# Linear attention and two MLPs in one program: batch 7's attention moved into a pair of the second layer, and q's products of batches 2 to 6 in three float32r passes

## The chip, the cores and the metric

The kernel is one program on one core of a Trainium2 chip. A core has a matrix engine (TensorE, PE in the rows; PEld is its weight load), a vector engine (VectorE, DVE), a scalar engine (ScalarE, ACT), GpSimd (POOL) and SyncE (SP), which here issues most of the DMAs. The metric is the time of one execution on the device in microseconds (us); lower is better.

## What is computed

Eight batches of eight heads, 576 tokens of 64 columns each, go through a linear attention with a root-mean-square norm. Its result, 4608 x 512, goes through two MLPs of width 2048:

```python
kv = einsum('bhsd,bhse->bhde', k, v)
out = einsum('bhsd,bhde->bhse', q, kv)
x = out / sqrt(mean(out*out, -1) + 1e-6) * g_norm     # heads side by side: 4608 x 512
h = x @ w_in1;  g = where(h >= 1, h, where(h <= -1, 0, (h + 1)**2 / 4));  x = g @ w_out1
r = maximum(x @ w_in2, 0);  out = (r*r) @ w_out2
```

## The kernel before

**Number formats.** q, k, v and x are float32. A large product is made of three float32r passes: each operand is split into a high part (a cast, mostly on ACT) and a low part (the rest, a subtraction on DVE), and high times high, high times low and low times high are summed (`mm3`, `mm_group`). A matmul on float32 operands needs no parts and takes longer.

**The MLPs.** A block is one layer of one batch, 512 of its tokens; the 64 left over of all eight batches make one more batch, the ninth. Blocks of layer 1 for batches 0 to 4 go through both matrices (`h_stage`, `g_stage`, `out_stage`), batches 5 and 6 only through the first (`h_stage`). From there on two batches are one *pair*, n = 0 to 5: `PAIRS` holds (1,5), (2,0), (2,2), (1,7), (2,4), (2,6), the layer and the first batch. A pair's matrix product is done by Strassen's scheme in Winograd's form, with seven products of half size in the order 1, 6, 2, 7, 5, 4, 3. Each pair has a first phase (`in_phase`: four q of seven products of two tiles of 6 matmuls, tiles `ph`, matrix w_in) and a second one (`out_phase`: seven products of 8 steps, tiles `po`, matrix w_out). Weights come ready in DRAM (`wsd`), one `ws` tile for each product, loaded by SP through a ring of eight buffers, so some products ahead. The results of a second layer's pair (`ov`, four of them, `outputs`) are transposed on DVE and stored by SP, eight DMAs each; they are written in the next pair's first phase, at steps 0, 1, 5 and 9 of its 28 (`late`). x of the pair after is loaded and split by jobs in the second phase (`x2_jobs`).

**The attention.** Two heads form a head pair, four head pairs a batch. For each: `load_kv` and `load_q` (SP: k, v, their last 64 rows as `rest`, and q in four DMAs), `kv_stage` (k times v on PE, two head pairs at a time, copied into the two diagonal blocks of `kvbd`), `t_stage` (transpose of q on DVE), `o_stage` (PE: q times kv, two halves of 288 tokens, then squares and scaling on ACT, the low part of the square on DVE), `r_stage` (PE: sums of squares by `ones`, two halves `pr`; ACT: logarithm, exponential, square; DVE: a Newton step for each half and the norm). Batch 1 uses three passes for q times kv; batches 2 to 7 use one matmul in float32 on q as it is transposed. The result becomes x of the MLP. For batch 7, whose MLP comes late, it is kept in DRAM (`keep_x`: `xpd`, and `xrd` for the 64 tokens left over).

**What sets the order.** The program is written as one list. Blocks are steps of `h_stage`; attention and the preparation of weights hang on them as hooks at numbered half steps. `STARTS` gives the starting slot s of each head pair of the list `order`; `attention` puts the loads at s - 7, kv and transpose at s, the halves at s + 3 and s + 4, the norm at s + 6. In the list before, batch 7's head pairs stand among those of batches 4, 5 and 6. In pairs there is no attention. A scheduler then orders each engine's instructions by their readiness in its own model; on the chip every engine executes its list in that order, and waits with all that is behind where an operand isn't there. Tiles live in rings and tagged buffers: a tile that takes over a buffer waits for the last reader of the one before, a store included.

Of the kernel before, what the change touches and what calls it, by code (L numbers as in the profile page):

```python
# [76 lines left out]
def linear_attention_rms_two_mlps(  # L77
# [12 lines left out]
    nc = tc.nc  # L90
# [18 lines left out]
    STARTS = (32, 39, 46, 53, 60, 66, 72, 78, 84, 90, 96, 102, 109, 115, 121, 127, 133, 139)  # L109
    STARTS += (145, 151, 156, 161, 166, 173)  # L110
# [30 lines left out]
    PAIRS = [(1, PLAIN), (2, 0), (2, 2), (1, B - 1), (2, 4), (2, 6)]  # L141
    LAST_B = B - 1
# [59 lines left out]
    kvbd = [const.tile([P, P], F32, name=f"kvbd{i}") for i in range(2)]  # L202
    kv1 = const.tile([P, 2, P], F32R, name="kv1")
# [271 lines left out]
    def kv_stage(*pairs):  # L475
        ps = bank(pairs[0][0], "pkv_{}_{}".format(*pairs[0]))
        for n, (b, hp) in enumerate(pairs):
            kt, vt = kvm.pop((b, hp))
            r = kvr.pop((b, hp))


            for c in range(MR + 1):
                for j in range(2):
                    s = slice(j * D, (j + 1) * D)
                    d = slice(n * P + j * D, n * P + (j + 1) * D)
                    lhs, rhs = (kt[:, c, j], vt[:, j, c, :]) if c < MR else (r[0][:, j], r[1][:, j])
                    nc.tensor.matmul(ps[s, d], lhs, rhs, start=c == 0, stop=c == MR)  # L487
        for n, (b, hp) in enumerate(pairs):
            for j in range(2):
                s = slice(j * D, (j + 1) * D)  # L490
                d = slice(n * P + j * D, n * P + (j + 1) * D)
                if b == 0:
                    copy(engine("kv_hi", b), kv0[s, hp, s], ps[s, d])
                    continue
                if (b, hp) in WHOLE:
                    copy(engine("kv_hi", b), kvw[s, hp % 2, s], ps[s, d])
                    continue
                if b > 1:
                    copy(engine("kv_hi", b), kvbd[turn[b, hp] % len(kvbd)][s, s], ps[s, d])
                    continue  # L500
                t = kv1
                copy(engine("kv_hi", b), t[s, 0, s], ps[s, d])
                nc.vector.tensor_tensor(t[s, 1, s], ps[s, d], t[s, 0, s].bitcast(F32), ALU.subtract)
# [56 lines left out]
    def t_stage(b, hp):  # L560
        work = [ap1.tile([P, S], F32, tag=f"wk{n}", name=f"wk{n}_{b}_{hp}") for n in range(2)]
        if b > 1 or (b, hp) in WHOLE:
            qT = ap1.tile([P, S], F32, tag="hl0", name=f"qT_{b}_{hp}")
            nc.vector.transpose(qT, qs.pop((b, hp)))
            hl[b, hp] = (work, qT)
            return
        qT = ap1.tile([P, S], F32, tag="wk2", name=f"qf_{b}_{hp}")
        parts = [ap1.tile([P, S], F32R, tag=f"hl{n}", name=f"qT{n}_{b}_{hp}") for n in range(2)]
        nc.vector.transpose(qT, qs.pop((b, hp)))
        copy(engine("q_hi", b), parts[0], qT)  # L570
        engine("q_lo", b).tensor_tensor(parts[1], qT, parts[0].bitcast(F32), ALU.subtract)
        hl[b, hp] = (work, parts)

    def o_stage(b, hp, half):
# [15 lines left out]
        if b > 1:  # L590
            nc.tensor.matmul(  # L591
                ps[:, :U], kvbd[turn[b, hp] % len(kvbd)], parts[:, c], start=True, stop=True
            )
        else:
            mm3(ps[:, :U], lambda a: kv1[:, a, :], lambda a: parts[a][:, c], True, True)
# [8 lines left out]
    def r_stage(b, hp):  # L604
# [24 lines left out]
        xt = st.tile([P, TB], F32, tag="st", name=f"xt_{hp}")  # L629
        nc.vector.scalar_tensor_tensor(t, t, -3.0, y, op0=ALU.add, op1=ALU.mult)  # L630
        nc.vector.tensor_tensor(xt, o[:, :TB], t[:, :TB], ALU.mult)
        xr = ap1.tile([P, REM], F32, tag="xr", name=f"xr_{hp}")
        nc.vector.tensor_tensor(xr, o[:, TB:], t[:, TB:], ALU.mult)
        x_kept[hp] = xt, xr
# [3 lines left out]
    def keep_x(b, hp):  # L638
        xt, xr = x_kept.pop(hp)
        nc.sync.dma_start(xpd[:, hp, :], xt)  # L640
        nc.sync.dma_start(xrd[:, hp, b, :], xr)
# [26 lines left out]
    def attention(starts, order):  # L668

        slots = []  # L670
        for j, (s, (b, hp)) in enumerate(zip(starts, order)):
# [3 lines left out]
            elif j % 2 == 0:  # L675
                two = order[j : j + 2]
                turn[two[1]] = len(turn)
                slots += [(max(0, s - 7), load_kv, *i) for i in two]
                slots.append((s, kv_stage, *two))
            slots += [  # L680
                (max(0, s - 7), load_q, b, hp),
                (s, t_stage, b, hp),
                (s + 3, o_stage, b, hp, 0),
                (s + 4, o_stage, b, hp, 1),
# [138 lines left out]
    t1_ring = Ring(*[(st, "st")] * 7, (dt, "dt3"))  # L823
    v_ring = Ring(*((wp, f"w0_{i}") for i in (12, 13)))
# [110 lines left out]

    FIRST = (1, 6, 5)
# [4 lines left out]
    def in_phase(n):  # L941
# [6 lines left out]
        for q in range(NQ):  # L948
            ps = {}
            e = {}  # L950
            for p in PRODUCTS:
                w = take_w2(layer(n), 0, q, p)
                for i in range(2):
# [11 lines left out]
                    if p == 1:  # L965
                        e[i, 1] = tile(e_ring, f"e1_{n}_{k}")
# [4 lines left out]
                    elif p in (6, 7):  # L971
                        kind = "e16" if p == 6 else "e167"
                        if p == 6:
                            e[i, 6] = tile(e_ring, f"{kind}_{n}_{k}")
                        else:
                            e[i, 7] = tile(e_ring, f"{kind}_{n}_{k}")
# [147 lines left out]
    def outputs(n, hn, hm):  # L1124
# [7 lines left out]
        t = (t_ring if n < NS - 1 else v_ring).tile([P, 2, TB], F32, f"ov{n}_{hn}_{hm}")  # L1132
# [96 lines left out]
    for t in kvbd + [kv1.bitcast(F32)]:  # L1229
        nc.vector.memset(t, 0.0)  # L1230
# [135 lines left out]
```

## Time and profile before

| | |
|---|---|
| runs | 1554.84, 1554.6, 1552.7 us; median 1554.6 |
| the profiled execution's own time | 1553.93 us |
| its span in the trace | 1552.2 us |
| the blocks end, pair 0's second phase begins | 630.16 us |
| pair 2, the second layer's second: first phase | 858.64 to 934.80 us |
| pair 2: second phase | 934.80 to 1010.96 us |
| granted clock of PE over the span | 1.00 |

All times in rows are from the start of the span. A row of the timeline joins instructions of the same kind that follow each other; xN is how many. In brackets stands how long the engine had stood idle before, and which instruction ended that. An L number is a line of the kernel's file, 246 being `mm3`, 927 `mm_group`, 591 the float32 product in `o_stage`, 487 `kv_stage` and 843 `load_w2`.

### The profile page before, as it was taken

The page shows a single profiled execution, that of the slowest core. Times are in us where ns is not written, and L with a number is a line of the kernel's source. Part 1 is how long each engine was busy: PE and PEld are TensorE (multiplying, and loading weights), DVE is VectorE, ACT ScalarE, POOL GpSimd, SP SyncE. Part 2 cuts the span into 40 slices and gives each one's busy share as a digit, 9 for nine tenths or more (in the row PEclk, how much of TensorE's full clock was granted, in tenths as well). Part 3 has the DMA queues.
Part 4 walks back from the last instruction along what each step waited for, and adds up shares of the span by engine and source line. Part 5 has one row for each costly group of instructions (what it writes and reads, how often), then busy time and mean ns, then how long its engine had stood idle before and what let it go on. Part 6 is the DMA issues. An engine that isn't in the chain of part 4 may idle for free.

```text
span 1552.2 us, 22204 instructions
## 1 busy us (share of the span) xinstructions
PE 1541.5 (99%) x7631; PEld 1274.0 (82%) x7633; DVE 1140.9 (74%) x1991; ACT 971.2 (63%) x1833; POOL 14.0 (1%) x38
## 2 busy tenths in 40 slices
PE   9999999999999999999999999999999999999999
PEld 5787888888788888888888888888888888888899
DVE  6986787777777866974597559778965596558666
ACT  5977677667667677654575466456646663666374
POOL 0000000000000000000000000000000000000000
PEclk9999999999999999999999999999999999999999
DMA  9666998998896944686576877687876676977796
GB/s 288 191 224 174 279 310 253 295 309 256 252 278 214 286 147 160 196 261 208 165 251 194 221 218 251 193 229 210 259 224 205 205 240 196 242 250 203 233 391 251
DMA packets 322431, 365.07 MB, mean 235 GB/s; under 512 B 197008, under 2 KB 222608, under 8 KB 322320
## 3 DMA queue, kind: packets, MB, share of 16 engines
q1 hardware_dynamic: 293472, 311.75, 67.6%
q10 hardware_dynamic: 28848, 51.91, 9.0%
q8 instruction: 61, 1.00, 0.3%
q14 instruction: 50, 0.41, 0.1%
HBM read 283.64 MB, written 79.95 MB: 234 GB/s over the span
## 4 chain that ended last, share of the span: by engine, by line
PE 96%; ACT 1%; DVE 1%; DMA 1%; issue 0%; ACTq 0%; DVEq 0%
PE po L927 32%; PE ph L927 27%; PE ph L246 18%; PE acc L246 14%; PE po L591 1%; PE pkv L487 1%; PE pr L616 1%; DMA x1d<-ev 1%; PE pwarm L1221 1%; DMA wt<-wsd 0%; ACT raw L276 0%; ACT w L225 0%; DVE t L530 0%; PE pr L545 0%; ACT u L726 0%
## 5 line engine op out<-in xcount | busy, mean ns | idle before, releaser
L927 PE MATMUL po<-t,ws 128*128 128x512 f32 x2016 | 457.9, 389 | 0.0
L927 PEld LDWEIGHTS po<-t,ws 128*128 128x128 f32 x2016 | 378.5, 188 | 78.5
L927 PE MATMUL ph<-x,ws 128*128 128x512 f32 (+1 forms) x2016 | 422.1, 371 | 0.0
L927 PEld LDWEIGHTS ph<-x,ws 128*128 128x128 f32 x2016 | 355.9, 188 | 65.5
L246 PE MATMUL ph<-x,w 128*128 128x512 f32 x1344 | 335.1, 397 | 1.4 <-ACT w L225 0.6
L246 PEld LDWEIGHTS ph<-x,w 128*128 128x128 f32 x1344 | 249.6, 188 | 57.6 <-ACT w L225 1.4
L856 DVE TENSOR_TENSOR t<-g,t 128x512 fp32r<-128x512 f32 (+1 forms) x336 | 216.8, 651 | 92.9 <-ACT t L225 91.1
L225 ACT CAST t<-g 128x512 fp32r<-128x512 f32 (+1 forms) x336 | 196.6, 590 | 122.4 <-DVE t L856 63.6
L984 DVE TENSOR_TENSOR h<-ph,e 128x512 f32<-128x512 f32 (+1 forms) x144 | 93.1, 646 | 68.2 <-PE ph L927 60.4
L246 PE MATMUL acc<-gs,w 128*128 128x512 f32 x528 | 133.6, 397 | 2.1 <-DVE u L728 1.6
L246 PEld LDWEIGHTS acc<-gs,w 128*128 128x128 f32 x528 | 98.1, 188 | 23.6 <-DVE u L728 2.0
L991 ACT ACTIVATE h<-h 128x512 f32<-128x512 f32 (+1 forms) x120 | 70.3, 585 | 60.1 <-DVE h L984 55.3
L246 PE MATMUL acc<-gs,wt 128*128 128x512 f32 x432 | 107.9, 397 | 0.0
L977 DVE TENSOR_TENSOR e<-ph,e 128x512 f32<-128x512 f32 (+1 forms) x96 | 61.0, 644 | 51.6 <-PE ph L927 50.8
L246 PEld LDWEIGHTS acc<-gs,wt 128*128 128x128 f32 x432 | 80.5, 188 | 17.4
L726 ACT ACTIVATE u<-ph,halfb 128x512 f32<-128x512 f32 x80 | 55.2, 690 | 53.4 <-PE ph L246 53.1
L728 DVE SCALAR_TENSOR_TENSOR u<-u,ph 128x512 f32<-128x512 f32 x80 | 54.6, 683 | 33.7 <-ACT u L232 33.5
L992 ACT ACTIVATE g<-h 128x512 f32<-128x512 f32 (+1 forms) x120 | 70.7, 589 | 3.2
L225 ACT CAST gs<-u 128x512 fp32r<-128x512 f32 x80 | 49.9, 623 | 36.1 <-DVE u L728 29.4
L225 ACT CAST x<-xr 128x512 fp32r<-128x512 f32 (+1 forms) x84 | 48.9, 585 | 37.5 <-DVE xr L907 19.6
L238 DVE TENSOR_TENSOR gs<-u,gs 128x512 fp32r<-128x512 f32 x80 | 54.8, 685 | 18.6 <-ACT gs L225 18.2
L991 ACT ACTIVATE u<-ph 128x512 f32<-128x512 f32 (+1 forms) x40 | 22.1, 553 | 62.6 <-PE ph L927 61.8
(144 smaller groups left out, 1597.6 us busy)
## 6 DMA issues: line engine op xcount, KB each, us to landing
ws<-wsd SPq DMA_DIRECT2D x364, 512.0 KB, 4.4
wsd<-s ACTq DMA_DIRECT2D x80, 512.0 KB, 4.3
wt<-wsd SPq DMA_DIRECT2D x36, 512.0 KB, 5.3
raw<-in_moe_w_in_dram SPq DMA_DIRECT2D x32, 512.0 KB, 5.5
raw<-in_moe_w_out_dram SPq DMA_DIRECT2D x32, 512.0 KB, 6.4
xr<-x1d SPq DMA_DIRECT2D x36, 256.0 KB, 4.8
out_dram<-ov SPq DMA_DIRECT2D x142, 64.0 KB, 4.0
wsd<-w SPq DMA_DIRECT2D x17, 512.0 KB, 4.5
```

Of the source, the lines that this page charges most:

```text
L225: return e.copy(dst, src)
L238: lo = engine(op + "_lo", phase).tensor_tensor(t[:, 1, :], src, t[:, 0, :].bitcast(F32), ALU.subtract)
L246: nc.tensor.matmul(dst, wt(a), xt(c), start=first and n == 0, stop=last and n == 2)
L487: nc.tensor.matmul(ps[s, d], lhs, rhs, start=c == 0, stop=c == MR)
L726: nc.scalar.activation(u, ps, AF.Relu, bias=halfb, scale=0.5)
L728: nc.vector.scalar_tensor_tensor(u, u, 1.0, ps, op0=ALU.min, op1=ALU.max)
L856: engine2(op + "_lo").tensor_tensor(t[:, 1, :], src, t[:, 0, :].bitcast(F32), ALU.subtract)
L927: nc.tensor.matmul(ps, wt(a), xt(c), start=first and n == 0 and i == 0, stop=last and n == len(lhs) - 1 and i == 2, skip_group_check=True,)
L977: nc.vector.tensor_tensor(e[i, p], bank, e[i, 1], ALU.add)
L984: nc.vector.tensor_tensor(h, bank, add, ALU.add)
L991: nc.scalar.activation(u, h, AF.Relu)
L992: nc.scalar.activation(g, u, AF.Square)
```

## The change

Batch 7 no longer stands in the list for the blocks: `STARTS` has 20 entries instead of 24, for batches 2 to 6. Its four head pairs run in pair 2 (`HOST`): `in_host` keeps their stages with the starts 0, 6, 12, 18, counted in steps of that pair's first phase; `host(i)` issues what is due. The loads of its first two head pairs (start minus 7) are due in the second phase of pair 1, the last store of its x in the second phase of pair 2. Its halves and its norm come one slot later, `keep_x` at s + 11.

Room for it: k and v of its second two head pairs take the four `dt` buffers, so `tmp` keeps three slots in that phase, and the two `at` banks leave the pairs' ring of PSUM banks. Sums of two tiles share one buffer (`keep_e`, tag `g`). kv of batch 7 has a float32 buffer of its own (`kv_host`). Its x and the 64 tokens left over become one tile `xt` in the ring `idle`, of two buffers, which also holds the four `ov` of pair 1; these are written at steps 0, 1, 3 and 4 of pair 2's first phase.

The products of q and kv of batches 2 to 6 go through `mm3`: `kvbd` holds a high and a low part, q is cast (ACT) and subtracted (DVE) after its transpose. Batch 7 keeps the float32 product.

```diff
-    STARTS = (32, 39, 46, 53, 60, 66, 72, 78, 84, 90, 96, 102, 109, 115, 121, 127, 133, 139)
-    STARTS += (145, 151, 156, 161, 166, 173)
+    STARTS = (32, 39, 46, 53, 61, 68, 75, 82, 92, 99, 106, 113, 122, 129, 136, 143)
+    STARTS += (151, 156, 161, 166)
...
-    kvbd = [const.tile([P, P], F32, name=f"kvbd{i}") for i in range(2)]
-    kv1 = const.tile([P, 2, P], F32R, name="kv1")
+    kvbd = [const.tile([P, 2, P], F32R, name=f"kvbd{i}") for i in range(2)]
+    kv_host = {}
...
+        if b == LAST_B and hp % 2 == 0:
+            t = ap2.tile([P, 2, P], F32, tag="xrem", name=f"kv_host_{hp}")
+            nc.gpsimd.memset(t, 0.0)
+            kv_host[hp // 2] = t
...
+                pool, tag = dt, f"dt{2 * hp + n - 4}"
...
-                if b > 1:
-                    copy(engine("kv_hi", b), kvbd[turn[b, hp] % len(kvbd)][s, s], ps[s, d])
+                if b == LAST_B:
+                    copy(engine("kv_hi", b), kv_host[hp // 2][s, hp % 2, s], ps[s, d])
                     continue
-                t = kv1
+                t = kvbd[turn[b, hp] % len(kvbd)]
                 copy(engine("kv_hi", b), t[s, 0, s], ps[s, d])
                 nc.vector.tensor_tensor(t[s, 1, s], ps[s, d], t[s, 0, s].bitcast(F32), ALU.subtract)
...
-        if b > 1 or (b, hp) in WHOLE:
+        if b == LAST_B or (b, hp) in WHOLE:
...
-        if b > 1:
+        if b == LAST_B:
             nc.tensor.matmul(
-                ps[:, :U], kvbd[turn[b, hp] % len(kvbd)], parts[:, c], start=True, stop=True
+                ps[:, :U], kv_host[hp // 2][:, hp % 2, :], parts[:, c], start=True, stop=True
             )
         else:
-            mm3(ps[:, :U], lambda a: kv1[:, a, :], lambda a: parts[a][:, c], True, True)
+            kv = kvbd[turn[b, hp] % len(kvbd)]
+            mm3(ps[:, :U], lambda a: kv[:, a, :], lambda a: parts[a][:, c], True, True)
...
-        xt = st.tile([P, TB], F32, tag="st", name=f"xt_{hp}")
         nc.vector.scalar_tensor_tensor(t, t, -3.0, y, op0=ALU.add, op1=ALU.mult)
-        nc.vector.tensor_tensor(xt, o[:, :TB], t[:, :TB], ALU.mult)
-        xr = ap1.tile([P, REM], F32, tag="xr", name=f"xr_{hp}")
-        nc.vector.tensor_tensor(xr, o[:, TB:], t[:, TB:], ALU.mult)
-        x_kept[hp] = xt, xr
+        xt = idle.tile([P, 2, TB], F32, f"xt_{hp}").rearrange("p a s -> p (a s)")
+        nc.vector.tensor_tensor(xt[:, :S], o, t, ALU.mult)
+        x_kept[hp] = xt
 
     x_kept = {}
 
     def keep_x(b, hp):
-        xt, xr = x_kept.pop(hp)
-        nc.sync.dma_start(xpd[:, hp, :], xt)
-        nc.sync.dma_start(xrd[:, hp, b, :], xr)
+        xt = x_kept.pop(hp)
+        nc.sync.dma_start(xpd[:, hp, :], xt[:, :TB])
+        nc.sync.dma_start(xrd[:, hp, b, :], xt[:, TB:S])
...
-                (max(0, s - 7), load_q, b, hp),
+                (max(0, s - 7) if b < LAST_B else s - 7, load_q, b, hp),
                 (s, t_stage, b, hp),
-                (s + 3, o_stage, b, hp, 0),
-                (s + 4, o_stage, b, hp, 1),
+                (s + 3 + (b == LAST_B), o_stage, b, hp, 0),
+                (s + 4 + (b == LAST_B), o_stage, b, hp, 1),
             ]
             if hp == 0 and b < LAST_B:
                 slots.append((s + 6, begin, b))
-            slots.append((s + 6, r_stage, b, hp))
+            slots.append((s + 6 + (b == LAST_B), r_stage, b, hp))
             if b == LAST_B:
-                slots.append((s + 8, keep_x, b, hp))
-            elif hp == NP - 1:
+                slots.append((s + 11, keep_x, b, hp))
...
+    idle = Ring(*((wp, f"w0_{i}") for i in (NF - 2, NF - 1)))
+    e_pairs = Ring(*[(gp, "g")] * 3)
+    banks_at = [(ps_t, "at")] * 2
...
+    def keep_e(n, e, i, p, k):
+
+        if n != HOST:
+            e[i, p] = e_ring.tile([P, TB], F32, f"e{p}_{n}_{k}")[:, : width(n)]
+        elif i == 0:
+            t = e_pairs.tile([P, 2, TB], F32, f"e{p}_{n}_{k}")
+            e[0, p], e[1, p] = t[:, 0], t[:, 1]
...
-        t = (t_ring if n < NS - 1 else v_ring).tile([P, 2, TB], F32, f"ov{n}_{hn}_{hm}")
+        ring = idle if n == HOST - 1 else t_ring if n < NS - 1 else v_ring
+        t = ring.tile([P, 2, TB], F32, f"ov{n}_{hn}_{hm}")
...
-    order = []
-    for b in range(2, LAST_B):
-        order += [(LAST_B, b - 4)] * (b >= 4) + [(b, hp) for hp in range(NP)]
-    order.append((LAST_B, NP - 1))
-    jobs += attention(STARTS, order)
+    jobs += attention(STARTS, [(b, hp) for b in range(2, LAST_B) for hp in range(NP)])
+    in_host = {}
+    for at, *job in attention((0, 6, 12, 18), [(LAST_B, hp) for hp in range(NP)]):
+        in_host.setdefault(at, []).append(job)
...
+    def host(i):
+        for at in sorted(a for a in in_host if a <= i):
+            for f, *a in in_host.pop(at):
+                f(*a)
+
     for n in range(NS + 1):
         step_in = in_phase(n) if n else ()
+        if n == HOST:
+            ps_ring.slots = [a for a in ps_ring.slots if a not in banks_at]
+            tmp.slots = [(ep, "e")] * 3
         for i, _ in enumerate(step_in):
+            if n == HOST:
+                host(i)
             pay(True)
-            if late and i in (0, 1, 5, 9) and n < NS:
+            if late and i in ((0, 1, 5, 9) if n != HOST else (0, 1, 3, 4)) and n < NS:
...
+        if n == HOST:
+            ps_ring.add(*banks_at)
+            tmp.slots = [a for i in range(3) for a in ((ep, "e"), (dt, f"dt{i}"))]
         result[n] = result_of(dict(g2))
         steps = start_out(n) if n else out_steps[0]
         if n < NS - 1:
-            for _ in steps:
+            for i, _ in enumerate(steps):
                 pay(True)
+                if n == HOST - 1 and i % 2 == 0:
+                    host(i // 2 - 7 * NQ)
+                elif n == HOST and i % 2 == 0:
+                    host(i // 2 + 7 * NQ)
```

Three places of the order, first of the kernel after, then of the one before. In the names, ph2_5_3 is pair 2's first phase, the bank opened by product 5, tile 3 of 8; ws2_0_1_3 is layer 2, first matrix, q = 1, product 3; x2_2_3_0 is x of pair 2 for product 3; 7_1 is batch 7, head pair 1.

**Place 1**, PE in pair 2's first phase, at the end of q = 1 (`ph2_5_3`, product 3) and the start of q = 2 (`ph2_1_4`):

```order
L936 MATMUL ph2_5_3_8883<-x2_2_3_0_8088,ws2_0_1_3_8689 128x512 x3

L494 MATMUL pkv_7_2_8930<-v_7_3_8729,k_7_3_8726 64x64 x8

L494 MATMUL pkv_7_2_8930<-rest1_128 64x64 x2

L936 MATMUL ph2_5_3_8883<-x2_2_3_1_8291,ws2_0_1_3_8689 128x512 x3

L624 MATMUL pr_7_1_1_8985<-s2_7_1_8864,ones_121 128x288

L624 MATMUL pr_7_1_1_8985<-s2lo_7_1_8901,ones_121 128x288

L598 MATMUL po_7_2_0_9066<-qT_7_2_8957,kv_host_2_8718 128x288

L936 MATMUL ph2_1_4_9005<-x2_2_1_0_7959,ws2_0_2_1_8737 128x512 x3

L936 MATMUL ph2_1_4_9005<-x2_2_1_1_8166,ws2_0_2_1_8737 128x512 x3

L936 MATMUL ph2_1_5_9016<-x2_2_1_0_7959,ws2_0_2_1_8737 128x512 x3

L936 MATMUL ph2_1_5_9016<-x2_2_1_1_8166,ws2_0_2_1_8737 128x512 x3

```

```order
L927 MATMUL ph2_5_2_8811<-x2_2_3_0_8132,ws2_0_1_3_8655 128x512 x3

L927 MATMUL ph2_5_2_8811<-x2_2_3_1_8335,ws2_0_1_3_8655 128x512 x3

L927 MATMUL ph2_5_3_8822<-x2_2_3_0_8132,ws2_0_1_3_8655 128x512 x3

L927 MATMUL ph2_5_3_8822<-x2_2_3_1_8335,ws2_0_1_3_8655 128x512 x3

L927 MATMUL ph2_1_4_8885<-x2_2_1_0_8003,ws2_0_2_1_8688 128x512 x3

L927 MATMUL ph2_1_4_8885<-x2_2_1_1_8210,ws2_0_2_1_8688 128x512 x3

```

The matmuls of product 3 and of the next product 1 stood next to each other; between them stand now the last sum of squares of head pair 1 and the first half of head pair 2. On DVE, at the same place (h and t1 are the pair's evictions and sums, t_7_1 and xt_1 the norm of head pair 1, qT_7_2 the transposed q of head pair 2):

```order
L997 TENSOR_TENSOR h2_3_3_8977<-ph2_5_3_8883,e6_2_2_8817 128x512

L1013 TENSOR_TENSOR t1_2_2_8997<-g2_2_2_0_8779 128x512

L1014 TENSOR_TENSOR g2_2_2_0_8779<-g2_2_2_1_8780,g2_2_2_0_8779 128x512

L537 SCALAR_TENSOR_TENSOR t_7_1_8990<-pr_7_1_0_8981,t_7_1_8990 128x288

L537 SCALAR_TENSOR_TENSOR t_7_1_8990<-pr_7_1_1_8985,t_7_1_8990 128x288

L1013 TENSOR_TENSOR t1_2_3_9000<-g2_2_3_0_8789 128x512

L637 SCALAR_TENSOR_TENSOR t_7_1_8990<-t_7_1_8990,wk0_7_1_8759 128x576

L1014 TENSOR_TENSOR g2_2_3_0_8789<-g2_2_3_1_8790,g2_2_3_0_8789 128x512

L639 TENSOR_TENSOR xt_1_8995<-wk1_7_1_8760,t_7_1_8990 128x576

L571 STREAM_TRANSPOSE qT_7_2_8957<-q_7_2_8732 128x576

L990 TENSOR_TENSOR e6_2_4_9035<-ph2_6_4_9028,e1_2_4_9012 128x512

```

```order
L984 TENSOR_TENSOR h2_3_2_8863<-ph2_5_2_8811,e16_2_2_8749 128x512

L984 TENSOR_TENSOR h2_3_3_8873<-ph2_5_3_8822,e16_2_3_8758 128x512

L1000 TENSOR_TENSOR t1_2_2_8877<-g2_2_2_0_8726 128x512

L1001 TENSOR_TENSOR g2_2_2_0_8726<-g2_2_2_1_8727,g2_2_2_0_8726 128x512

L1038 TENSOR_TENSOR g2_2_2_0_8726<-g2_2_2_1_8727,t1_2_2_8877 128x512

L1000 TENSOR_TENSOR t1_2_3_8880<-g2_2_3_0_8737 128x512

L1001 TENSOR_TENSOR g2_2_3_0_8737<-g2_2_3_1_8738,g2_2_3_0_8737 128x512

L856 TENSOR_TENSOR t2_1_3_9215<-g2_2_3_0_8737,t2_1_3_9215 128x512

L1038 TENSOR_TENSOR g2_2_3_0_8737<-g2_2_3_1_8738,t1_2_3_8880 128x512

L977 TENSOR_TENSOR e16_2_4_8916<-ph2_6_4_8909,e1_2_4_8892 128x512

```

The transpose stands behind the last step of head pair 1's norm.

**Place 2**, SP in the same phase: the weights of the end of q = 1, the stores of pair 1's results, the loads of head pairs 2 and 3.

```order
L1135 DMA out_0_dram<-ov1_0_1_8589 128x4x32 x8

L852 DMA ws2_0_1_7_8600<-wsd2_0_1_113 128x1024

L852 DMA ws2_0_1_5_8620<-wsd2_0_1_113 128x1024

L1135 DMA out_0_dram<-ov1_1_0_8637 32x16x32 x8

L852 DMA ws2_0_1_4_8648<-wsd2_0_1_113 128x1024

L1135 DMA out_0_dram<-ov1_1_1_8678 32x16x32 x8

L852 DMA ws2_0_1_3_8689<-wsd2_0_1_113 128x1024

L441 DMA rest0_127<-in_k_dram 64x2x64

L441 DMA rest0_127<-in_v_dram 64x2x64

L434 DMA k_7_3_8726<-in_k_dram 128x8x64

L441 DMA rest1_128<-in_k_dram 64x2x64

L437 DMA v_7_3_8729<-in_v_dram 128x2x256

```

```order
L1122 DMA out_0_dram<-ov1_0_1_8582 128x4x32 x8

L843 DMA ws2_0_1_7_8593<-wsd2_0_1_113 128x1024

L843 DMA ws2_0_1_5_8613<-wsd2_0_1_113 128x1024

L843 DMA ws2_0_1_4_8631<-wsd2_0_1_113 128x1024

L843 DMA ws2_0_1_3_8655<-wsd2_0_1_113 128x1024

L1122 DMA out_0_dram<-ov1_1_0_8677 32x16x32 x8

L843 DMA ws2_0_2_1_8688<-wsd2_0_2_114 128x1024

```

Two weights, ws2_0_1_4 and ws2_0_1_3, stood ahead of the store of ov1_1_0; each now stands behind a store, and the loads of batch 7 behind them.

**Place 3**, DVE at the step to pair 2's second phase (t2_1_0, t2_1_1 are low parts that the second phase's first product multiplies):

```order
L997 TENSOR_TENSOR h2_4_7_9343<-ph2_6_7_9225,e1_2_6_9200 128x512

L537 SCALAR_TENSOR_TENSOR t_7_3_9318<-pr_7_3_0_9309,t_7_3_9318 128x288

L537 SCALAR_TENSOR_TENSOR t_7_3_9318<-pr_7_3_1_9313,t_7_3_9318 128x288

L997 TENSOR_TENSOR h2_3_6_9355<-ph2_5_6_9287,e6_2_6_9223 128x512

L637 SCALAR_TENSOR_TENSOR t_7_3_9318<-t_7_3_9318,wk0_7_3_9121 128x576

L997 TENSOR_TENSOR h2_3_7_9365<-ph2_5_7_9298,e6_2_6_9223 128x512

L639 TENSOR_TENSOR xt_3_9323<-wk1_7_3_9122,t_7_3_9318 128x576

L865 TENSOR_TENSOR t2_1_0_9375<-g2_2_0_0_8546,t2_1_0_9375 128x512

L1013 TENSOR_TENSOR t1_2_6_9369<-g2_2_6_0_9201 128x512

```

```order
L984 TENSOR_TENSOR h2_4_7_9163<-ph2_6_7_9074,e1_2_7_9059 128x512

L984 TENSOR_TENSOR h2_3_6_9175<-ph2_5_6_9123,e16_2_6_9072 128x512

L984 TENSOR_TENSOR h2_3_7_9185<-ph2_5_7_9134,e16_2_7_9081 128x512

L1000 TENSOR_TENSOR t1_2_6_9189<-g2_2_6_0_9049 128x512

L1001 TENSOR_TENSOR g2_2_6_0_9049<-g2_2_6_1_9050,g2_2_6_0_9049 128x512

L856 TENSOR_TENSOR t2_1_5_9237<-g2_2_5_0_8904,t2_1_5_9237 128x512

L1000 TENSOR_TENSOR t1_2_7_9192<-g2_2_7_0_9060 128x512

```

In the kernel before, these rows hold the low part of the sixth tile (t2_1_5), that of the first having been made further ahead; now the first stands behind xt_3, the end of batch 7's last norm.

## Rows read from the trace of the kernel before

**Rows 1.** the page: busy us of each engine, share of the span, instructions
```profile
PE 1541.5 (99%) x7631; PEld 1274.0 (82%) x7633; DVE 1140.9 (74%) x1991; ACT 971.2 (63%) x1833; POOL 14.0 (1%) x38
```

**Rows 2.** the chain in order of time: start us, us, what
```profile
89.47 0.61 PE po L246 x4
...
146.54 0.97 PE po L591 x4
...
177.45 1.31 PE pkv L487 x40
...
630.16 76.16 PE po L927 x336
...
858.64 76.16 PE ph L927 x336
```

**Rows 3.** stretch; us, busy of PE PEld DVE ACT POOL, PEclk, DMA share, GB/s
```profile
858.60:934.60 76.00, 76.00 (x337) 62.96 (x336) 43.24 (x66) 44.42 (x74) 0.00 (x0) 1.00 0.79 220
```

**Rows 4.** timeline of PE, batch 1: start, us, line, op, shapes, [idle before <-releaser]
```profile
117.15 0.69 PE L246 MATMUL po<-qT,kv 128*128 128x288 f32 x4
117.67 1.09 PE L246 MATMUL acc<-gs,w 128*128 128x512 f32 x4
```

**Rows 5.** timeline of PE, its longest waits in two stretches of the blocks
```profile
54.46 0.96 PE L246 MATMUL acc<-gs,w 128*128 128x512 f32 x3 [1.55 <-DVE u L728]
...
399.34 0.75 PE L591 MATMUL po<-qT,kvbd 128*128 128x288 f32 x2 [1.12 <-DVE t L530]
```

**Rows 6.** timeline from 574 us: batch 6, from the sum of squares to t
```profile
578.00 0.42 PE L616 MATMUL pr<-s2lo,ones 128*128 128x288 f32 x2
...
578.33 0.50 ACT L617 ACTIVATE wk<-pr,lnb 128x288 f32<-128x288 f32 x1 [1.33 <-PE pr L616]
...
579.25 0.49 ACT L617 ACTIVATE wk<-pr,lnb 128x288 f32<-128x288 f32 x1
...
580.14 0.78 ACT L619 ACTIVATE wk<-wk,expb 128x576 f32<-128x576 f32 x1
...
580.96 0.69 ACT L232 ACTIVATE t<-wk 128x576 f32<-128x576 f32 x1
...
581.73 0.82 DVE L530 SCALAR_TENSOR_TENSOR t<-pr,t 128x288 f32<-128x288 f32 x2 [0.76 <-ACT t L232]
...
583.86 0.75 DVE L534 TENSOR_TENSOR t<-wk,t 128x576 f32<-128x576 f32 x1
```

**Rows 7.** line L564: ns min/median/max, first and last start us
```profile
L564 DVE STREAM_TRANSPOSE qT<-q x26: 766/774/779, 54.3 to 572.4; 128x576 f32<-128x576 f32 x26
```

**Rows 8.** timeline of SP's queue in pair 2's first phase
```profile
872.98 2.93 SPq L843 DMA_DIRECT2D ws<-wsd  x4
876.00 8.59 SPq L1122 DMA_DIRECT2D out_dram<-ov  x8
...
886.62 7.53 SPq L1122 DMA_DIRECT2D out_dram<-ov  x8
```

**Rows 9.** timeline of SP's queue in the blocks
```profile
458.64 0.62 SPq L434 DMA_DIRECT2D rest<-in_k_dram  x1
```

**Rows 10.** DMA issues by line: count, KB each, median us to landing
```profile
ws<-wsd SPq DMA_DIRECT2D x364, 512.0 KB, 4.4
...
xpd<-xt SPq DMA_DIRECT2D x4, 256.0 KB, 5.3
...
rest<-in_v_dram SPq DMA_DIRECT2D x28, 32.0 KB, 3.3
```

**Rows 11.** timeline across the step from pair 2's first phase to its second
```profile
934.64 3.33 PE L927 MATMUL po<-t,ws 128*128 128x512 f32 x14
...
934.91 0.69 DVE L984 TENSOR_TENSOR h<-ph,e 128x512 f32<-128x512 f32 x1 [0.67 <-ACT h L991]
...
936.20 0.62 ACT L225 CAST t<-g 128x512 fp32r<-128x512 f32 x1
...
936.94 0.69 DVE L856 TENSOR_TENSOR t<-g,t 128x512 fp32r<-128x512 f32 x1
```

More of the change, by code (lines that the diff above doesn't have):

```diff
@@ L141, in linear_attention_rms_two_mlps @@
     PAIRS = [(1, PLAIN), (2, 0), (2, 2), (1, B - 1), (2, 4), (2, 6)]
+    HOST = 2
     LAST_B = B - 1
@@ L421, in load_kv @@
             pool, tag = (ep, "e") if (b, hp) == (0, NP - 1) else (st, "st")
+            if b == LAST_B and hp > 1:
+                pool, tag = dt, f"dt{2 * hp + n - 4}"
             t = pool.tile([P, TB], F32, tag=tag, name=f"{'kv'[n]}_{b}_{hp}")
@@ L677, in attention @@
                 turn[two[1]] = len(turn)
-                slots += [(max(0, s - 7), load_kv, *i) for i in two]
+                slots += [(s - 7, load_kv, *i) for i in two]
                 slots.append((s, kv_stage, *two))
             slots += [
-                (max(0, s - 7), load_q, b, hp),
+                (max(0, s - 7) if b < LAST_B else s - 7, load_q, b, hp),
                 (s, t_stage, b, hp),
-                (s + 3, o_stage, b, hp, 0),
-                (s + 4, o_stage, b, hp, 1),
+                (s + 3 + (b == LAST_B), o_stage, b, hp, 0),
+                (s + 4 + (b == LAST_B), o_stage, b, hp, 1),
             ]
@@ L687, in attention @@
                 slots.append((s + 6, begin, b))
-            slots.append((s + 6, r_stage, b, hp))
+            slots.append((s + 6 + (b == LAST_B), r_stage, b, hp))
             if b == LAST_B:
-                slots.append((s + 8, keep_x, b, hp))
-            elif hp == NP - 1:
+                slots.append((s + 11, keep_x, b, hp))
+            if b < LAST_B and hp == NP - 1:
                 slots.append((max(2 * NF * b, 0) if b < PLAIN + 1 else s + 9, store_xrem, b))
@@ L965, in in_phase @@
                     if p == 1:
-                        e[i, 1] = tile(e_ring, f"e1_{n}_{k}")
+                        keep_e(n, e, i, 1, k)
                         g2[k] = [
@@ L971, in in_phase @@
                     elif p in (6, 7):
[L972 to L976, printed above, removed]
+                        keep_e(n, e, i, p, k)
                         nc.vector.tensor_tensor(e[i, p], bank, e[i, 1], ALU.add)
@@ L1228, in linear_attention_rms_two_mlps @@
         nc.vector.memset(ones[s, s].bitcast(F32), 1.0 / D)
-    for t in kvbd + [kv1.bitcast(F32)]:
-        nc.vector.memset(t, 0.0)
+    for t in kvbd:
+        nc.vector.memset(t.bitcast(F32), 0.0)
     for t in rests:
```

## The prediction

> **What bounds the kernel now.** Read first the engine totals [rows 1]: TensorE (PE) is busy 99% of the span, 1541.5 of 1552.2 us. Then the chain that ended last, in order of time [rows 2]: from 630.16 us on it is PE alone, each phase of a pair 336 matmuls in 76.16 us (630.16 and 858.64 stand for all), 0.2267 us for one matmul of 512 columns and 2.72 us for the 12 of one product. So there is nothing to win in the pairs; any wait that PE gets there is paid in full, and before 630 us PE's own work counts. Third, the stretch of the pair that will be the host [rows 3]: PE 76 of 76 us, VectorE (DVE) 43.2, ScalarE (ACT) 44.4. By shares there is room for batch 7: each of its head pairs takes about 4 us of DVE (one transpose [rows 7], 0.82 for two half steps and 0.75 [rows 6] for each of three more) and 6 of ACT (the four of [rows 6] are 2.5, six more on halves by 0.5 as its logarithms, and copies). Shares don't decide here, though: PE executes in its written order, and the written order at two places makes it wait for a whole chain of the other engines.
>
> **The change part by part.**
>
> *Three float32r passes instead of one float32 matmul, batches 2 to 6.* On the chain the two halves of one head pair cost 0.97 us in float32 (146.54), 0.485 us a half. A three-pass product of 288 columns stands in the trace too, in batch 1: four passes start at 117.15 and the next matmul at 117.67 [rows 4], 0.13 us a pass, six for a head pair 0.79 us. The saving is 0.18 us a head pair, 20 x 0.18 = 3.6 us. On the other side stand passes that had to wait: four took 0.61 us at 89.47 [rows 2], six 0.91 us, and the saving would be 1.2 us. I take 3.6, since the scheduler sets the passes with the low part 0 to 5 matmuls behind the high one. What the passes need (a cast on ACT, a subtraction of 576 and two of 64 columns on DVE for each head pair) lies beside PE's work: four head pairs of about 4 us DVE and 6 us ACT leave the same blocks. I cost it at nothing; were it uncovered, one late low part would cost what the batch 1 row shows, 0.1 us a head pair.
>
> *Batch 7 out of the blocks and into pair 2.* PE's work moves one to one (two kv stages, eight float32 halves, eight sums of squares) and I cost it at nothing. What its absence may give back is waiting: the largest wait of PE in the blocks is 1.12 us [rows 5], and all of them after 90 us I put at no more than 3 us. I count 0, because such waits come as much from weight preparation as from attention.
>
> *The wait at po_7_2_0 (place 1 of the order).* PE has pr_7_1_1, the sum of squares of head pair 1, and right behind it po_7_2_0, which needs qT_7_2. On DVE qT_7_2 stands behind xt_1, which is the end of the chain that pr_7_1_1 only begins: logarithm, exponential, square on ACT, then two steps of 288, two of 576 on DVE, and the transpose. How long that takes is in the trace [rows 6]: last pr at 578.00, t finished at 583.86 + 0.75 = 584.61, 6.6 us, and the transpose 0.77 [rows 7], 7.4 us. Of the two logarithms only the second hangs on pr_7_1_1 (0.9 us less, 578.33 to 579.25), and two more sums of 512 columns stand between (about 0.5 net, one of them beside ACT's work): 7.0 us. Behind po_7_2_0 on PE all of the next product queues, so PE stands still. Bounds: 6.5 and 7.4.
>
> *The loads in front of it (place 2).* The weights ws2_0_1_3 stood ahead of the store of ov1_1_0 on SP; now they stand behind both ov1_1_0 and ov1_1_1, whose transposes DVE does only after q=0's last product and after head pair 0's norm. Eight such stores hold SP for 8.59 and 7.53 us [rows 8]. From the phase's start (0): PE is through the seventh product at 1.3 (kv stage, 177.45 [rows 2]) + 7 x 2.72 + 0.97 = 21.3, ov1_1_0 is transposed to its first half at 23.0, its stores end at 30.5, one weight load, ov1_1_1 until 38.5, ws2_0_1_3 issued until 38.9, landed 4.4 later [rows 10]: 43.3. PE wants it at 1.3 + 13 x 2.72 + 2.5 (po, pr, po) = 39.2. In the kernel before, the four loads at 872.98 [rows 8] include it: 17 us after that phase began at 858.64, with 18 us to spare. Behind it come four loads of rests, k and v: 0.6 us of SP each [rows 9], the last issued at 42.7, landed 3.3 later [rows 10] at 46.0; PE needs them for the second kv stage, which in its order lies within this product. pr_7_1_1 then runs at about 47.4 instead of 43.5: 3.9 us. Bounds: 0, if the stores go out faster than SP's rows show, and 6, with 8.6 us for each. ws2_0_2_1, issued behind four q loads (by 0.6 as well) at 45.4, lands at 49.8 and is hidden behind the 7.0 us. First wait together: 10.9 us.
>
> *The step from pair 2's first phase to its second (place 3).* Before, the high and low parts of the first t tiles were made ahead of the phase's end, and PE went from 858.64's phase to the next without a gap (858.64 + 76.16 = 934.80). Now `g` is held by the e pairs until the last eviction, and DVE has the norm of head pair 3 among the last evictions. Before, the last one began 0.27 us after the step (934.91 against 934.64, [rows 11]). Now it waits behind two 288 steps and one of 576, which wait for ACT: about 0.7; then xt_3 and the low part of t2_1_0 follow, ready at 0.7 + 0.6 + 0.7 + 0.7 = 2.7, where PE needs it at 0.45. The next lows come 1.2 us apart (one other sum of 0.6 between). The fourth tile, t2_1_3, takes over xt_3's buffer and so waits for its store: xt_3 ready at 2.1, landed 5.3 later [rows 10], cast 0.62 and low part 0.69 (936.94): 9.1. From there PE has 0.9 + 4 x 1.36 us left of the product and ends at 15.5 instead of 8 x 1.36 = 10.9: 4.6 us. Bounds: 1.8 (the eviction at 0.27 and no wait for the store) and 6.2 (ACT 1.5 us later).
>
> **Sum.** -3.6 + 10.9 + 4.6 = +11.9 us on the profiled execution's own 1553.93 us: 1565.8. The median of the three runs is 1554.6, 0.7 above the profiled one; I predict 1566 us. The bounds add to +2.7 (-3.6 - 2 + 6.5 + 1.8) and +18.4 (-1.2 + 13.4 + 6.2).
>
> **Rivals.**
> 1. *The loads are in time, only the chains wait.* For it: SP's long rows contain waits for queue space, which more distant stores would not have. Against: the same stores took 7.5 to 8.6 us in this very phase before. 1565.8 - 3.9 = 1562.
> 2. *The clock falls.* PE never stood still for more than 1.55 us in the rows read [rows 5], and the granted clock is 1.00 in the host's stretch [rows 3], so no row shows what 10 us of waiting do. If the level of 1.2 GHz is granted after it, each product costs 2.72 us more until 2.4 GHz comes back. With one to two products 1565.8 + 2.7 to 5.4, about 1570. The Trainium skill ("TensorE: Matmul & The Clock Gate", part 1 on the HAM clock gate) states this rule: the array drops to the lower level when it has idled and gets the upper one back only by sustained matmuls; by it rival 2 would be the rule here, and no run so far shows it.
> 3. *Batch 7 hides in pair 2, and the time falls.* DVE and ACT are idle 43% and 42% of the host stretch [rows 3]; if PE's idle time in pair 2's two phases stays under the 3.6 us that the passes save, the kernel is not slower. With the waits of the blocks also gone it would end at 1553.9 - 3.6 - 0 to 3, about 1549. Against: po_7_2_0 follows pr_7_1_1 directly, and 6.5 us of dependent instructions lie between them whatever the load; that alone exceeds 3.6.
> 4. *The passes save nothing.* Low parts late as at 89.47, saving 1.2 or less, with new waits in the blocks of 1 to 2 us: 1565.8 + 2.4 + 1.5, about 1570. For it: DVE gets 20 x 1.15 = 23 us more of parts (one subtraction of 576 by 0.75, two small ones by 0.2); against it: it loses 4 x 4 = 16 us of batch 7, and ACT loses more than it gets.
>
> **How the numbers follow.** Forecast (both waits, clock kept) 0.56; rival 1 0.12; rival 2 0.16; rival 3 0.09; rival 4 0.07. A measurement of this kernel can tell about 0.2% from no change, 3.1 us. Rival 3 gives faster 0.04 and same 0.05; the low end of rival 1 and of the bounds gives another 0.05 of same. Slower: 0.86. The range goes from 1557, the sum with all the lower bounds (1553.9 + 2.7), which leaves out rival 3, to 1574, which takes in rivals 2 and 4 and most of the upper bound.
>
> **What would show it.** In the profile after: the first phase of pair 2 about 20 us longer than 76.16 (9 us of it moved work), PE idle before po_7_2_0 with the DVE transpose as what ended it, about 7 us; PE idle of some 4 us just ahead, ended by a DMA of ws or rest; PE idle at the start of the next phase ended by DVE's t (L865) or ACT's cast, 4 to 5 us; the float32r po of 288 columns at 0.13 us a pass and the end of the blocks at about 618 us. I am wrong if the phases of pair 2 show PE without gaps, if the blocks end later than 621 us, or if the granted clock of the stretch behind the wait is under 1.

## The result and the profile after

The changed kernel takes 1561.92 us (median of 6 runs, 1561.38 to 1562.01), the kernel before beside it 1554.07 (6 runs, 1552.6 to 1555.35). The ratio is 1.0051 with a 95% interval of 1.0038 to 1.0064: 7.9 us slower, where the prediction had 11.9 more, at 1566. The profiled execution took 1561.38 us, its span is 1559.6, 7.4 more than before.

The engine totals, on the page of the changed kernel:

```profile
PE 1540.5 (99%) x7671; PEld 1274.8 (82%) x7673; DVE 1160.7 (74%) x2046; ACT 978.2 (63%) x1853; POOL 14.3 (1%) x40
```

PE is busy for 1.0 us less than in [rows 1], while the span is 7.4 longer: PE stands idle for 8.4 us more. (Matmuls at a lower clock count as busy; they come up below.) The chain in order of time says where (start us, us, what):

```profile
614.09 76.16 PE po L936 x336
690.25 76.16 PE ph L936 x336
766.41 76.16 PE po L936 x336
842.57 1.31 PE pkv L494 x40
...
886.53 7.76 DMA ws<-wsd
894.33 0.75 DVE xt L639
895.08 0.70 DVE qT L571
895.91 1.30 PE po L598 x2
...
1018.12 21.99 PE ph L936 x97
```

The blocks end at 614.09 instead of 630.16 [rows 2], 16.1 us earlier. In pair 2 DVE and a weight load stand on the chain, where it was PE alone. That load held nothing up: DVE's instruction before xt ran from 893.73 to 894.42, so DVE was not idle there. By the starts of the phases the 7.45 us are these: blocks -16.07 (613.93 against 630.00), pair 2's first phase +20.33 (96.49 us from 842.41, the end of pair 1's last product, to 938.90, against 76.16), its second phase +2.89 (79.05), the second phase of pair 3 +0.30.

PE's timeline around place 1, the row of `po` standing for po_7_2_0 (columns as in the rows of before):

```profile
882.57 0.69 PE L494 MATMUL pkv<-v,k 128*64 128x64 f32 x16 [0.44 <-ACT wk L218]
883.56 0.40 PE L624 MATMUL pr<-s,ones 128*128 128x288 f32 x1 [0.31 <-ACT wk L218]
...
888.90 0.29 PE L624 MATMUL pr<-s2lo,ones 128*128 128x288 f32 x1
895.91 1.30 PE L598 MATMUL po<-qT,kv_host 128*128 128x288 f32 x2 [6.72 <-DVE qT L571]
896.60 3.62 PE L936 MATMUL ph<-x,ws 128*128 128x512 f32 x9
```

The wait is there as forecast: 6.72 us, ended by the transpose. What the prediction put ahead of it, 3.9 us of late loads, is not: no wait is ended by a DMA. Only 0.75 us are lost there, on ACT. SP's queue shows why (start us, us of SP, count); these rows answer to [rows 8]:

```profile
865.58 5.15 SPq L1135 DMA_DIRECT2D out_dram<-ov  x8
870.83 0.46 SPq L852 DMA_DIRECT2D ws<-wsd  x1
872.65 4.13 SPq L1135 DMA_DIRECT2D out_dram<-ov  x8
876.88 0.44 SPq L852 DMA_DIRECT2D ws<-wsd  x1
```

The stores start when the prediction said (23.2 us after the phase's start), but eight take 5.15 and 4.13 us instead of about 7.5. ws2_0_1_3 is out at 34.9 us instead of 38.9. In the kernel before, four weight loads go out right ahead of each of the two groups of stores [rows 8], and one store of each group is long (start us, us of SP):

```profile
879.13 3.83 SPq L1122 DMA_DIRECT2D out_dram<-ov  x1
```
```profile
889.90 2.62 SPq L1122 DMA_DIRECT2D out_dram<-ov  x1
```

Most others take about 0.5. The long ones end, at 882.96 and 892.52, when the last of those four loads lands (883.03 and 892.54). In the changed kernel at most one weight load is under way when a group begins.

In exchange something stands behind the wait that only a rival had. Three stretches of the changed kernel (us; busy of PE, PEld, DVE, ACT, POOL; granted clock; DMA share; GB/s):

```profile
880.00:889.00 9.00, 8.13 (x66) 5.49 (x64) 3.87 (x7) 7.72 (x20) 0.00 (x0) 1.00 0.92 250
896.00:899.20 3.20, 3.20 (x8) 2.44 (x9) 0.00 (x0) 1.10 (x3) 0.00 (x0) 0.51 0.87 283
899.20:935.00 35.80, 35.80 (x161) 29.55 (x160) 17.45 (x28) 21.61 (x43) 0.00 (x0) 1.00 0.65 189
```

For 3.2 us after the wait PE has 0.51 of the clock, the level of 1.2 GHz, and its matmuls come 0.427 us apart instead of 0.227. Against the upper level some 1.6 us are lost there (3.2 us at half). The level fell while PE stood still: it is 1.00 from 889.2 to 892.2 and 0.50 from 892.3 to 895.9. The Trainium skill ("TensorE: Matmul & The Clock Gate", part 1) states that the array drops to the lower level when it has idled and gets the upper one back by sustained matmuls. The trace agrees, with a wait of 6.72 us and 3.2 us of matmuls before the upper level was back.

The step to pair 2's second phase, first PE's timeline, then DVE's:

```profile
938.90 0.73 PE L936 MATMUL po<-t,ws 128*128 128x512 f32 x2
941.34 21.02 PE L936 MATMUL po<-t,ws 128*128 128x512 f32 x88 [1.70 <-DVE t L865]
```
```profile
939.33 0.68 DVE L997 TENSOR_TENSOR h<-ph,e 128x512 f32<-128x512 f32 x1
939.93 0.74 DVE L639 TENSOR_TENSOR xt<-wk,t 128x576 f32<-128x576 f32 x1
940.60 0.68 DVE L865 TENSOR_TENSOR t<-g,t 128x512 fp32r<-128x512 f32 x1
...
945.42 0.68 DVE L865 TENSOR_TENSOR t<-g,t 128x512 fp32r<-128x512 f32 x1
```

Where [rows 11] shows PE without a gap, it now waits 1.70 us for the first low part, which stands behind xt_3 on DVE; the fourth, at 945.42, costs it only a few tenths more.

### The profile page after: what moved, and what is told of

Same layout as the page of the kernel before. It is cut to its first block, busy times and chain, and to the rows that moved or that the text cites. A ratio compares the mean times of both kernels' runs of the same rounds, so it can differ in the third digit from the quotient of the medians.

```text
span 1559.6 us, 22360 instructions
## 1 busy us (share of the span) xinstructions
PE 1540.5 (99%) x7671; PEld 1274.8 (82%) x7673; DVE 1160.7 (74%) x2046; ACT 978.2 (63%) x1853; POOL 14.3 (1%) x40
## 4 chain that ended last, share of the span: by engine, by line
PE 96%; ACT 2%; DVE 1%; DMA 1%; issue 0%; SPq 0%; ACTq 0%; DVEq 0%
PE po L936 32%; PE ph L936 27%; PE ph L247 19%; PE acc L247 14%; PE pkv L494 1%; PE po L247 1%; PE pr L624 1%; DMA ws<-wsd 0%; PE po L598 0%; DMA v<-in_v_dram 0%; PE pwarm L1234 0%; ACT raw L277 0%; ACT w L226 0%; DMA xr<-xrd 0%; PE pr L552 0%
## 5 line engine op out<-in xcount | busy, mean ns | idle before, releaser
L936 PE MATMUL ph<-x,ws 128*128 128x512 f32 (+1 forms) x2016 | 427.8, 373 | 0.0
L247 PE MATMUL ph<-x,w 128*128 128x512 f32 x1344 | 327.4, 392 | 1.3 <-ACT w L226 0.6
```

What stands on the lines that cost most here:

```text
L247: nc.tensor.matmul(dst, wt(a), xt(c), start=first and n == 0, stop=last and n == 2)
L936: nc.tensor.matmul(ps, wt(a), xt(c), start=first and n == 0 and i == 0, stop=last and n == len(lhs) - 1 and i == 2, skip_group_check=True,)
```

## The experiments

Each ran beside the kernel before: its median was 1553.66 us beside passes_only, host_only, q_earlier and last_earlier, 1553.12 beside t_ahead and spread, 1554.07 beside the changed kernel. Phases are counted as above, from the first matmul of one to that of the next; pair 2's first begins where pair 1's last product ends, so the kv stage at its head belongs to it. They come from one profiled execution of each kernel.

| | median us | ratio to before (95%) | pair 0's second phase starts | pair 2, first phase | second phase |
|---|---|---|---|---|---|
| before | | 1 | 630.00 | 76.16 | 76.16 |
| changed | 1561.92 | 1.0051 (1.0038 to 1.0064) | 613.93 | 96.49 | 79.05 |
| passes_only | 1552.68 | 0.9991 (0.9982 to 1.0000) | 628.77 | 76.16 | 76.16 |
| host_only | 1564.81 | 1.0069 (1.0057 to 1.0082) | 616.76 | 96.71 | 79.61 |
| q_earlier | 1555.53 | 1.0012 (1.0003 to 1.0021) | 614.58 | 90.55 | 79.35 |
| t_ahead | 1559.45 | 1.0037 (1.0025 to 1.0050) | 614.64 | 92.95 | 80.82 |
| last_earlier | 1559.17 | 1.0033 (1.0021 to 1.0046) | 613.97 | 96.95 | 76.84 |
| spread | 1549.61 | 0.9977 (0.9968 to 0.9987) | 613.82 | 86.84 | 77.74 |

**The two halves of the change.** `passes_only`, from the kernel before:

```diff
...
-        if b > 1 or (b, hp) in WHOLE:
+        if (b, hp) in WHOLE:
...
-        if b > 1:
-            nc.tensor.matmul(
-                ps[:, :U], kvbd[turn[b, hp] % len(kvbd)], parts[:, c], start=True, stop=True
-            )
-        else:
-            mm3(ps[:, :U], lambda a: kv1[:, a, :], lambda a: parts[a][:, c], True, True)
+        kv = kvbd[turn[b, hp] % len(kvbd)]
+        mm3(ps[:, :U], lambda a: kv[:, a, :], lambda a: parts[a][:, c], True, True)
...
```

> The kernel before with three float32r passes for all of batches 2 to 7 (24 head pairs) and batch 7 left in the blocks. Theory (the passes save 0.16 us a head pair, and the 4.6 us of waits that the blocks lost came from batch 7's absence): 3.8 us less than before, 1550 us, blocks end at 626. Rival A (half of those waits were the float32 product's own and go with it): 1547 to 1548 us. Rival B (the parts come late with batch 7 still there): within 1 us of before.

It took 1.0 us off by the medians, and the blocks end 1.2 us earlier, for 24 head pairs: rival B. PE's longer waits in its blocks from 60 us on (us, times, longest), and below them those of the kernel before:

```profile
PE ph L245 <- DVE u L720: 3.9, 3, 1.6
PE ph L245 <- ACT w L224: 0.2, 1, 0.2
```
```profile
PE po L591 <- DVE t L530: 1.1, 1, 1.1
PE acc L246 <- ACT ev L781: 0.5, 1, 0.5
PE ph L246 <- ACT w L225: 0.2, 1, 0.2
```

The wait of 1.1 us went with the float32 product, but 3.9 us of others came: `ph` waits for a PSUM bank that DVE evicts (`u`) late. All of PE from 90 us to the blocks' end says the same: its busy time falls by 3.6 us (537.99 to 534.36), 0.15 a head pair, and its idle time grows from 2.0 to 4.4.

`host_only`, from the changed kernel:

```diff
...
-        if b == LAST_B or (b, hp) in WHOLE:
+        if b > 1 or (b, hp) in WHOLE:
...
+        elif b > 1:
+            nc.tensor.matmul(
+                ps[:, :U], kvbd[turn[b, hp] % len(kvbd)], parts[:, c], start=True, stop=True
+            )
         else:
...
```

> The changed kernel with the products of batches 2 to 6 back in one float32 matmul. Theory (passes save 3.2 us, the blocks' waits are gone for batch 7's absence): 1565 us, blocks end at about 617. Rival A (the waits come back with the float32 product): 1567 to 1569 us.

1564.81, as the theory said. Its blocks end at 616.76, so in batch 7's absence the passes save 2.83 us, 0.14 a head pair; with batch 7 there, 1.2. PE's idle time from 90 us to the blocks' end is 0.2 us in both kernels without batch 7, so there nothing eats the saving. That DVE, which makes the low parts, has the room only when batch 7 is gone fits this. But batches 2 to 6 also got new starts in `STARTS`, and no run parts the two. The absence, with these starts, shortens the blocks by 13.24.

**What the wait at po_7_2_0 is.** `q_earlier`:

```diff
-                (max(0, s - 7) if b < LAST_B else s - 7, load_q, b, hp),
+                (max(0, s - 7) if b < LAST_B else s - 7 - 3 * (hp > 1), load_q, b, hp),
```

> The changed kernel with the q loads of head pairs 2 and 3 of batch 7 three steps earlier, so ahead of the two late stores on SP; the order then has qT_7_2 before xt_0 on DVE and po_7_2_0 three products behind pr_7_1_1. Theory (PE stood still for 6.7 us because po_7_2_0 hung on a transpose queued behind head pair 1's norm, and the 2 us at the level of 1.2 GHz behind it came from that wait): both go, 8.7 us less; a new wait of 2 to 3 us before pr_7_2_0, which now stands right behind po_7_2_1: about 1556 us, granted clock near 1.00 in the whole phase. Rival (the loads are what is late; the wait only changes its name and is then ended by a DMA of ws or rest): 1560 us or more.

1555.53. The scheduler, which reckons with the loads, now set the transpose ahead of xt_0 and po_7_2_0 three products later; the wait of 6.72 us is gone, the granted clock is 1.00 from 842.6 to 933.6, and the first phase is 5.9 us shorter. The new wait came where it was expected, a little smaller:

```profile
897.88 1.13 PE L598 MATMUL po<-qT,kv_host 128*128 128x288 f32 x4
900.24 0.40 PE L624 MATMUL pr<-s,ones 128*128 128x288 f32 x1 [1.23 <-ACT wk L218]
901.23 0.40 PE L624 MATMUL pr<-s,ones 128*128 128x288 f32 x1 [0.60 <-ACT wk L218]
```

This doesn't yet tell whether the wait was the transpose's alone. `t_ahead` leaves PE and SP as they are and moves only the transpose on DVE, ahead of the norm and of two of the pair's sums:

```diff
...
+            turned[b, hp] = nc.vector.transpose(qT, qs.pop((b, hp)))
...
+            if (b, hp) == (LAST_B, 1):
+                with tc.issue_after(turned[b, 2].ins):
+                    newton(t[:, c], m)
...
+                if (n, q) == (HOST, 1):
+                    with tc.issue_after(turned[LAST_B, 2].ins):
+                        sums_in(n, 2 * q + i)
...
```

> The changed kernel with one thing moved: on DVE the transpose qT_7_2 stands ahead of the norm of head pair 1 (t_7_1) and of two sums of q = 1. PE's order and SP's order are as in the changed kernel, po_7_2_0 still directly behind pr_7_1_1. Theory A (the prediction's: the wait is for the transpose, queued behind the norm): the transpose runs at about 889.4, po_7_2_0 about 6 us earlier, and the lower clock behind the wait goes too: 1554 us. Theory B (po_7_2_0 also takes over the PSUM bank of pr_7_1_0, which is free only when DVE's first Newton step has read it, behind logarithm, exponential and square): 2.5 to 4 us of wait remain, now ended by DVE's L637 or L537, and the clock's part may remain: 1557 to 1559 us. Rival (the q load lands too late for either): no gain, 1562 us.

1559.45: theory B, half a microsecond over its range. The transpose ran at 889.97, and PE still waited, now for the Newton step (timelines of PE and of DVE):

```profile
889.61 0.29 PE L626 MATMUL pr<-s2lo,ones 128*128 128x288 f32 x1
893.03 0.72 PE L600 MATMUL po<-qT,kv_host 128*128 128x288 f32 x2 [3.13 <-DVE t L537]
```
```profile
889.97 0.77 DVE L573 STREAM_TRANSPOSE qT<-q 128x576 f32<-128x576 f32 x1
892.43 0.82 DVE L537 SCALAR_TENSOR_TENSOR t<-pr,t 128x288 f32<-128x288 f32 x2 [1.69 <-ACT t L233]
```

po_7_2_0 takes the PSUM bank of pr_7_1_0: there are two for the attention, and the Newton step reads the sum out of it. So 3.6 of the 6.72 us were the transpose's place, 3.13 the bank's, and directly behind pr_7_1_1 no place on DVE would have been early enough. The clock fell for this shorter wait too, 1.5 us after PE went on:

```profile
894.00:900.00 6.00, 6.00 (x21) 4.77 (x21) 3.52 (x6) 2.17 (x5) 0.00 (x0) 0.72 1.01 300
```

**The step.** `last_earlier`:

```diff
-    for at, *job in attention((0, 6, 12, 18), [(LAST_B, hp) for hp in range(NP)]):
+    for at, *job in attention((0, 6, 12, 17), [(LAST_B, hp) for hp in range(NP)]):
```

> The changed kernel with head pair 3 of batch 7 started at step 17 instead of 18. Place 1 stands as it was; at the step to the second phase the norm of head pair 3 ends before the last four evictions. Theory (the 3.6 us at the step come from DVE's norm standing among the last evictions): about 3 us less, 1559 us, with the wait of 6.7 us before po_7_2_0 unchanged. Rival (the wait is for buffers: g of the e pairs, and xt_3's store): no gain, 1562 us.

1559.17, 2.75 less by the medians. The profiled execution, the slowest of the five, took 1.55 less: the second phase gains 2.2, the first loses 0.5, since the lower clock behind its wait of 6.72 us lasted to 900.6, and 0.5 more went in pair 1's second phase, at 814. xt_3 now ends at 937.41, and the first low part comes ahead of the last evictions (timelines of DVE and of PE):

```profile
936.66 0.75 DVE L639 TENSOR_TENSOR xt<-wk,t 128x576 f32<-128x576 f32 x1
937.42 0.69 DVE L997 TENSOR_TENSOR h<-ph,e 128x512 f32<-128x512 f32 x1
938.03 0.68 DVE L865 TENSOR_TENSOR t<-g,t 128x512 fp32r<-128x512 f32 x1
```
```profile
939.87 4.86 PE L936 MATMUL po<-t,ws 128*128 128x512 f32 x20
944.94 5.29 PE L936 MATMUL po<-t,ws 128*128 128x512 f32 x22 [0.21 <-DVE t L865]
```

So most of the step's loss was the norm's place among the evictions, and little of it the buffers.

**All together.** `spread` has both edits of numbers above and one more:

```diff
-            if late and i in ((0, 1, 5, 9) if n != HOST else (0, 1, 3, 4)) and n < NS:
+            if late and i in ((0, 1, 5, 9) if n != HOST else (0, 1, 4, 7)) and n < NS:
```

> The changed kernel with three numbers changed: the q loads of head pairs 2 and 3 three steps earlier, head pair 3 started at 17, the late stores at steps 0, 1, 4 and 7 instead of 0, 1, 3 and 4. The order then has two products between pr_7_1_1 and po_7_2_0, and four between po_7_2_1 and pr_7_2_0. Theory (waits of PE in pair 2 arise where its order puts a dependent step right behind the one before, not from load): of the 14.6 us of waits in pair 2 some 1.5 us remain, and the granted clock stays 1.00: 1549 us, faster than before. Rival (the two PSUM banks of the attention or the later stores make new waits): 1552 to 1554 us.

1549.61 us, 0.23% less than the kernel before (interval 0.13 to 0.32%): faster than both kernels. Of PE's waits in pair 2's first phase and the step one is listed (first fence), though the second phase is still 1.6 us over 76.16, in waits of 0.3 us and less, and pair 3's second phase 0.4; the second is PE's timeline at place 1:

```profile
PE po L936 <- DVE t L865: 0.3, 1, 0.3
```
```profile
887.64 0.30 PE L624 MATMUL pr<-s2lo,ones 128*128 128x288 f32 x1
887.77 5.62 PE L936 MATMUL ph<-x,ws 128*128 128x512 f32 x24
893.24 1.13 PE L598 MATMUL po<-qT,kv_host 128*128 128x288 f32 x4
```

Between pr_7_1_1 and po_7_2_0 there are 24 matmuls of the pair, 5.4 us, in which DVE and ACT do what PE waited for.

## Why the prediction was right, and where it was off

The direction, the place of the main wait and what ended it were right; the time lies in the range, 4.1 us under the forecast. `spread` gives the measure for the terms: its first phase is 86.84 us with no listed wait, so batch 7's own work takes up to 10.7 there, not 9. What is over that is waiting and the lower clock.

| term | forecast | measured | from |
|---|---|---|---|
| passes | -3.6 | -2.8 | host_only's blocks against the changed kernel's |
| waits that the blocks lose | 0 | -2.5 | 13.24 (host_only) less 10.7 of moved work |
| first wait, places 1 and 2, with the clock behind it | +10.9 | +9.65 | 96.49 against spread's 86.84 |
| step, place 3 | +4.6 | +3.2 | 79.05 - 76.16, and 0.3 in pair 3 |
| sum | +11.9 | +7.5 | the spans differ by 7.4 |

- *Passes.* The mechanism held and its size was near. "Lies beside PE's work" held only because batch 7 had left: `passes_only` shows 3.9 us of new waits where it stays.
- *Blocks costed at nothing.* This is the mis-sized term that moved the sum most. The prediction saw up to 3 us there and counted none, since weight preparation might keep the waits. Its lower bound had 2 of them. They went with batch 7 and the new starts: PE's idle time in the blocks from 90 us on is 2.0 us in the kernel before and 0.2 in `host_only`. So 1.8 of the 2.5 are seen in the trace; the other 0.7 rest on the moved work costing the same in both places, which no run shows.
- *First wait.* The sum came out near, by two errors that cancelled. The loads (3.9) failed: they were taken from stores that lasted 7.5 to 8.6 us in the kernel before, where each group stood behind four weight loads; without these it took 4 to 5, and no wait for a DMA came. Rival 1 had this right, long stores that contain waits, but distance isn't the reason that the rows show: the second group follows the first by 2 us in either kernel. Against the 3.9 stand 1.6 us of the lower clock, rival 2, which the forecast left out, and 0.75 of waits for ACT. 6.72 + 1.6 + 0.75 = 9.1 of the 9.65; the rest is in no listed wait.
- *The chain behind the 7.0.* Its length was right, 6.72, but it wasn't the only reason: the bank of pr_7_1_0, which the prediction didn't see, would have held PE for 3.13 us without it.
- *Step.* The first low part was ready 2.4 us after the step (forecast 2.7). The wait for xt_3's store came to a few tenths instead of dominating: the fourth low part was ready at 7.2 us (946.1), not 9.1.
- *Luck, and its own signs.* The measured 1561.92 is rival 1's time (1562, chance 0.12), and that is chance too: rival 1 has neither the lower clock nor the waits that the blocks lost. Of the prediction's signs, the 20 us, the 7 us and the transpose came; the 4 us ended by a DMA didn't, and the step's wait was 1.70 us instead of 4 to 5. One sign of being wrong came true: a granted clock under 1 behind the wait.
- *Rival 3*, that batch 7 hides in pair 2, was wrong for this order and right for the idea: in `spread` it does, and the time falls.

## What to carry to other kernels

Idle shares of the other engines say that work fits, not that it is free: look in the written order of the bounding engine for two dependent steps that stand next to each other, and add up what runs between them. Such a place can come from a transfer that the scheduler reckons late and that isn't late on the chip; the q load of `q_earlier` had landed by 885.7 in the changed kernel, and its transpose ran at 895.0. Three numbers, for the q loads, the start of head pair 3 and the stores, were worth 12 us here. And take two reasons for a wait into account, the operand and the buffer that it is written to: an experiment that moves only one of them tells them apart.

## What the runs showed of the hardware

The granted clock went to the level of 1.2 GHz within a wait of 6.72 us (0.50 from 892.3), and 1.5 us behind one of 3.13 (0.72 over 894 to 900). After waits of 1.70 us it did either: in `q_earlier` it stayed at 1.00 (933 to 950), in `t_ahead` it was 0.50 from 938.9 to 942.3. There a wait of 3.13 us lay some 45 us back; in the changed kernel one of 6.72 us lay as far back, and behind its 1.70 us the clock stayed at 1.00 (941.3 to 950). So the runs don't show what decides it. Some 1.6 of the changed kernel's lost microseconds belong to a wait and are not in the waiting time itself.
